# Half of a pair's VectorE background work put ahead of the pair's evacuation

## The chip, the cores and the metric

One core of one Trainium2 chip. The metric is the device time of the kernel in microseconds. A run of one core has no second die to compare with, so a run counts as fast when it is within 1.5% of the fastest of its kernel. Engines: PE is TensorE, DVE is VectorE, ACT is ScalarE, POOL is GpSimd, SP is SyncE.

## The reference

Input x is 2048 tokens of 576 features in bf16. It is normalised, and three things are added: x itself, a diagonal complex state-space layer (576 states, a scan over the 2048 tokens) and a gated unit with a hidden width of 4608.

```python
xn = _layernorm(x, axis=-1)
# _A_ref: Bu = xn @ B_bar^T (complex); h_t = Lam_bar * h_{t-1} + Bu_t; y = 2 Re(h C^T) + xn * Dskip
# _B_ref: (sigmoid(xn @ w_gate) * (xn @ w_up)) @ w_down
return x + _A_ref(xn, ...) + _B_ref(xn, ...)
```

## The kernel before

The tokens are four blocks of 512; two blocks make a half. For each half the hidden width is done in three slots of twelve 128-wide slices, so there are six stages. A stage first runs its **gate/up groups** (18 matmuls into one pair of PSUM banks, "pgu"; ACT makes a sigmoid and a copy, DVE multiplies them). Now and then a **state-input group** ("pbu") stands between them; ACT copies it into the SBUF tiles bure and buim. Then come the **down-projection pairs** ("pd"): two token tiles of 128 at a time, which DVE adds to an accumulator. In the third and sixth stage the pairs also carry the state terms and write the output.

All PSUM tiles rotate through four slots of two banks. Everything else that DVE has to do (tables, the scan, norms, residuals) is background work. It is a queue of items with estimated costs; at set points of the program `bg.step(us)` hands out credit, and as many items as the credit pays for are placed there in DVE's program.

```python
    def step(self, us):                      # class Background
        self.now += 1
        self.credit = min(self.credit + us, 5.0)
        while True:
            q = self.head()
            if q is None or q[0][0] > self.credit:
                return
            cost, fn, _ = q.popleft()
            self.credit -= cost
            fn()
# ... cut
psum = ctx.enter_context(tc.tile_pool(name="psum", bufs=PE_SLOTS, ...))    # PE_SLOTS = 4
# ... cut
        def evac(self):                      # class StateIn
            bre = ssmp.tile([P, TB], FP32, name="bure", tag="bure", bufs=2)
            bim = ssmp.tile([P, TB], FP32, name="buim", tag="buim", bufs=2)
            if self.pt < PT:
                nc.scalar.copy(bre[:], self.ps[:, 0, :])
                nc.scalar.copy(bim[:], self.ps[:, 1, :])
                bg.step(T_GROUP - 0.1)
# ... cut
    def ssm_w(nb, pt, part):                 # a background item; part 1 is the last reader of bre and bim
        bre, bim = bu[(nb, pt)]
        # ... cut
        a, b = (bre, bim) if part == 0 else (bim, bre)
        tq = bft("tq", 2)
        nc.vector.tensor_mul(w, t1, a[:])
        nc.vector.tensor_mul(tq[:], t2, b[:])
        # ... cut
# ... cut
    def d_pair(tts, terms, final, free=False):
        n = len(terms[0])                    # 12 terms; 21 in the stages with state terms
        pds = [ps_pair("pd") for _ in tts]
        # ... cut: the matmuls of the pair
        for tt, pd in zip(tts, pds):
            acc = accs[tt]
            if final:
                ob = lnp.tile([P, D], BF16, name="ob", bufs=2)
                nc.vector.tensor_add(halves(ob[:]), halves(acc[:]), pd[:, :, 0:DH])
                nc.sync.dma_start(o[tt * P:(tt + 1) * P, :], ob[:])
            else:
                nc.vector.tensor_add(halves(acc[:]), halves(acc[:]), pd[:, :, 0:DH])
        if free:
            acc_free[0] = tts[1] + 1
        for _ in tts:
            bg.step(n * T_DTERM - 0.76 - 0.2)
```

## Time and profile before

| | before |
|---|---|
| time, median of 3 runs | 507.96 us (507.86 to 508.02) |
| span of the profiled run | 505.8 us |
| PE busy | 499.5 us, 99% |
| DVE busy | 322.5 us, 64% |
| ACT busy | 204.5 us, 40% |
| PE's share of the chain that ended last | 98% |
| waits of PE that the trace names | 1.2 + 1.2 + 0.9 us |

How to read it: the chain is followed back from the last instruction, at each step to what released it. A kernel whose chain is 98% PE is as long as PE's work plus PE's gaps. Idle time on DVE counts only where PE or the end waits for it.

### The profile page before, as it was taken

The numbers are of one execution on the slowest core, as the hardware profiler recorded it, in microseconds if no ns is written. First come the engines' busy times: TensorE is split into PE (matmuls) and PEld (weight loads), VectorE is DVE, ScalarE is ACT, GpSimd is POOL, SyncE is SP. The second block draws the span as 40 slices with busy tenths as digits, with TensorE's granted clock in tenths as the row PEclk, the third lists the DMA queues.
The fourth block names the chain that finished last, engine by engine and source line by source line (L and its number), as shares of the span: only waits on it lengthen the run. The fifth ranks groups of instructions, "written<-read, shape, count | busy, mean of one in ns | idle before, by whom it ended". The sixth has DMA issues, their size and how long they took to land.

```text
span 505.8 us, 13370 instructions
## 1 busy us (share of the span) xinstructions
PE 499.5 (99%) x5892; PEld 311.6 (62%) x5892; DVE 322.5 (64%) x706; ACT 204.5 (40%) x368; POOL 90.8 (18%) x134
## 2 busy tenths in 40 slices
PE   8999999999999999999999999999999999999997
PEld 5544675444477444477764555985555985557995
DVE  6889679887868787847589767579675222221111
ACT  4955733556500756530025655005655005553000
POOL 7116320123200043110000331100431001300000
PEclk9999999999999999999999999999999999999999
DMA  8999694155220096232170661200643201600001
GB/s 212 208 162 247 134 192 100 27 139 141 49 49 27 2 189 155 61 88 73 48 143 1 165 141 49 49 16 10 162 103 88 50 25 30 184 1 1 26 25 49
DMA packets 40960, 45.77 MB, mean 90 GB/s; under 512 B 28614, under 2 KB 32326, under 8 KB 40902
## 3 DMA queue, kind: packets, MB, share of 16 engines
q0 software_dynamic: 10608, 34.22, 28.1%
q1 hardware_dynamic: 29862, 10.37, 11.0%
q8 instruction: 46, 0.75, 0.6%
q10 hardware_dynamic: 432, 0.33, 0.2%
q14 instruction: 12, 0.10, 0.1%
HBM read 34.36 MB, written 2.36 MB: 73 GB/s over the span
## 4 chain that ended last, share of the span: by engine, by line
PE 98%; DMA 1%; DVE 1%; ACT 0%; issue 0%; ACTq 0%
PE pgu L502 55%; PE pd L616 33%; PE pbu L531 7%; PE pd L576 1%; PE pd L584 1%; DMA xt<-in_A_x_dram 1%; PE ptr L780 0%; DVE bnst L230 0%; PE pgu L772 0%; ACT buim L538 0%; DVE xn L255 0%; DVE mv L231 0%; DVE ob L585 0%; PE ptr L196 0%; ACT bure L537 0%
## 5 line engine op out<-in xcount | busy, mean ns | idle before, releaser
L502 PE MATMUL pgu<-xT,wgu 64*128 64x512 bf16 (+1 forms) x2628 | 284.0, 373 | 1.2 <-ACT buim L538 1.2
L502 PEld LDWEIGHTS <-wgu 64*128 64x128 bf16 x2628 | 138.2, 94 | 141.5 <-issue 1.4
L616 PE MATMUL pd<-wd,hT 64*128 64x288 bf16 x2208 | 140.7, 283 | 0.0
L508 ACT ACTIVATE sT<-pgu 128x512 bf16<-128x512 f32 x144 | 86.5, 601 | 118.5 <-PE pgu L502 117.5
L616 PEld LDWEIGHTS <-hT 64*128 64x128 bf16 x2208 | 116.4, 94 | 20.0
L511 DVE TENSOR_TENSOR hT<-sT,uT 128x512 bf16<-128x512 bf16 x144 | 60.6, 422 | 84.3 <-ACT uT L509 84.2
L509 ACT CAST uT<-pgu 128x512 bf16<-128x512 f32 x144 | 84.2, 585 | 0.0
L154 POOL DMA_DIRECT2D wgu<-in_B_w_gate_dram x36 | 27.6, 766 | 228.4 <-PE pgu L502 216.6
L626 DVE TENSOR_TENSOR acc<-acc,pd 128x576 f32<-128x576 f32 x32 | 22.7, 750 | 35.9 <-PE pd L616 35.9
L160 POOL DMA_DIRECT2D wd<-in_B_w_down_dram x36 | 26.4, 735 | 104.5 <-PE pd L616 104.4
L537 ACT COPY bure<-pbu 128x512 f32<-128x512 f32 x16 | 9.4, 585 | 86.0 <-PE pbu L531 68.6
L623 DVE TENSOR_TENSOR ob<-acc,pd 128x576 bf16<-128x576 f32 x14 | 9.9, 751 | 41.8 <-PE pd L616 41.8
L531 PE MATMUL pbu<-xT,bt 64*128 64x512 bf16 x288 | 33.8, 376 | 0.0
L616 PEld LDWEIGHTS <-hst 64*128 64x128 bf16 x504 | 26.4, 94 | 4.5
L616 PE MATMUL pd<-ctre,hst 64*128 64x288 bf16 x224 | 28.8, 283 | 0.0
L616 PE MATMUL pd<-ctim,hst 64*128 64x288 bf16 x224 | 28.8, 283 | 0.0
L154 POOL DMA_DIRECT2D wgu<-in_B_w_up_dram x36 | 26.5, 737 | 1.8 <-DMA wgu<-in_B_w_up_dram 1.8
L445 DVE TENSOR_TENSOR_SCAN gre<-r,g0re,wrim 128x512 bf16<-128x512 f32 x20 | 25.6, 1279 | 0.1
L531 PEld LDWEIGHTS <-bt 64*128 64x128 bf16 x288 | 14.6, 94 | 15.9
L452 DVE TENSOR_TENSOR_SCAN gim<-r,g0im,wrim 128x512 bf16<-128x512 f32 x16 | 20.3, 1272 | 0.0
L230 DVE BATCH_NORM_STATS2 bnst<-xt 128x6 f32<-128x288 bf16 x32 | 12.5, 432 | 2.6 <-DMA xt<-in_A_x_dram 2.6
L432 DVE TENSOR_TENSOR tq<-T,buim 128x512 bf16<-128x512 bf16 x20 | 13.7, 685 | 0.0
(126 smaller groups left out, 292.9 us busy)
## 6 DMA issues: line engine op xcount, KB each, us to landing
wgu<-in_B_w_gate_dram POOLq DMA_DIRECT2D x36, 288.0 KB, 4.2
wgu<-in_B_w_up_dram POOLq DMA_DIRECT2D x36, 288.0 KB, 4.9
wd<-in_B_w_down_dram POOLq DMA_DIRECT2D x36, 288.0 KB, 4.9
out_dram<-ob SPq DMA_DIRECT2D x15, 144.0 KB, 1.9
xt<-in_A_x_dram SPq DMA_DIRECT2D x10, 144.0 KB, 3.4
xt<-in_A_x_dram POOLq DMA_DIRECT2D x4, 144.0 KB, 7.0
bt<-ctre POOLq DMA_DIRECT2D x2, 288.0 KB, 6.2
bt<-ctim POOLq DMA_DIRECT2D x2, 288.0 KB, 8.1
```

Source lines behind the costliest of these rows:

```text
L154: eng.dma_start(w[rows, :, :], src[:, fs].rearrange("(c p) f -> p c f", p=H))
L160: nc.gpsimd.dma_start(wd[:], B_w_down[f0:f0 + FP * P, :].rearrange("(n p) d -> p n d", p=P))
L432: nc.vector.tensor_mul(tq[:], t2, b[:])
L445: nc.vector.tensor_tensor_scan(gre[:], r_bc, w[:, 0, :], g0re[:, col], ALU.mult, ALU.add)
L452: nc.vector.tensor_tensor_scan(gim[:], r_bc, w[:, 1, :], g0im[:, col], ALU.mult, ALU.add)
L502: nc.tensor.matmul(self.ps[:, gi, cols], w[rows, c, fs], xT[self.nb][rows, c, cols], start=c == 0, stop=c == NH - 1)
L508: nc.scalar.activation(sT[:], self.ps[:, 0, :], ACT.Sigmoid)
L509: nc.scalar.copy(uT[:], self.ps[:, 1, :])
L511: nc.vector.tensor_mul(h[:], sT[:], uT[:])
L531: nc.tensor.matmul(out, w, xT[self.nb][rows, c, ts_], start=c == 0, stop=c == NH - 1)
L616: m = nc.tensor.matmul(pds[k][:, a, 0:DH], lhsT[rows, :], rhs[rows, a * DH:(a + 1) * DH], start=turn == 0 and i == 0, stop=turn == 1 and i ...
L626: nc.vector.tensor_add(halves(acc[:]), halves(acc[:]), pd[:, :, 0:DH])
```

## The change

The intent: in DVE's program the evacuation stands ahead of the background work, so in the kernel before DVE stands idle until the pair's matmuls are done and does its background work only afterwards. With one of the two steps ahead of the evacuation, that share fills the idle time.

```diff
+        bg.step(n * T_DTERM - 0.76 - 0.2)
         for tt, pd in zip(tts, pds):
             acc = accs[tt]
             if final:
@@
         if free:
             acc_free[0] = tts[1] + 1
-        for _ in tts:
-            bg.step(n * T_DTERM - 0.76 - 0.2)
+        bg.step(n * T_DTERM - 0.76 - 0.2)
```

## The prediction

> **What bounds the kernel now.** I read the engine totals first, then the chain of waits that ended last, then the waits of each engine, and last the timeline around the only gap that is left. The page of the kernel before:
>
> ```profile
> span 505.8 us, 13370 instructions
> PE 499.5 (99%) x5892; PEld 311.6 (62%) x5892; DVE 322.5 (64%) x706; ACT 204.5 (40%) x368; POOL 90.8 (18%) x134
> PEclk9999999999999999999999999999999999999999
> PE 98%; DMA 1%; DVE 1%; ACT 0%; issue 0%; ACTq 0%
> ```
>
> TensorE (PE) runs for 499.5 of 505.8 us at the full granted clock, and 98% of the chain is PE. VectorE (DVE) is busy 64% of the time and 1% of the chain. So the most that any reordering of VectorE work can win is PE's idle time, 505.8 - 499.5 = 6.3 us. The waits of PE say what it is made of:
>
> ```profile
> engine line waited for: us in total, times, longest us
> PE pgu L772 <- DVE warm L182: 1.2, 1, 1.2
> PE pgu L502 <- ACT buim L538: 1.2, 1, 1.2
> PE ptr L780 <- DVE rstd L238: 0.9, 1, 0.9
> ```
>
> Two of the three (1.2 and 0.9 us) lie in the first 7 us, before any pair. After PE's last matmul come about 3 us of last evacuation and store (505.8 - 502.9). That leaves one gap that background work can touch: 1.2 us, when a gate/up matmul of line 502 waited for ScalarE (ACT) to copy out "buim". 1.2 + 0.9 + 1.2 + 3.0 = 6.3, so nothing is left over.
>
> The waits of VectorE show why the change was thought of:
>
> ```profile
> DVE ob L623 <- PE pd L616: 41.8, 7, 8.9
> DVE acc L626 <- PE pd L616: 35.9, 14, 4.5
> ```
>
> VectorE sits idle 77.7 us at the evacuations of the down-projection pairs (lines 623 and 626), waiting for PE to finish the pair. But it is VectorE that waits; no row says that PE waits for these evacuations.
>
> Now the gap. The timeline of the three engines around it:
>
> ```profile
> 265.43 5.99 PE L502 MATMUL pgu<-xT,wgu 64*128 64x512 bf16 x54
> 272.58 3.63 PE L502 MATMUL pgu<-xT,wgu 64*128 64x512 bf16 x32 [1.15 <-ACT buim L538]
> ...
> 265.53 0.58 ACT L509 CAST uT<-pgu 128x512 bf16<-128x512 f32 x1
> 271.45 0.58 ACT L537 COPY bure<-pbu 128x512 f32<-128x512 f32 x1 [5.34 <-PE pgu L502]
> 271.93 0.59 ACT L538 COPY buim<-pbu 128x512 f32<-128x512 f32 x1
> ...
> 259.81 1.42 DVE L623 TENSOR_TENSOR ob<-acc,pd 128x576 bf16<-128x576 f32 x2 [1.04 <-PE pd L616]
> 261.15 0.45 DVE L270 TENSOR_TENSOR tmpxd<-xn,dskip_rows 128x576 bf16<-128x576 bf16 x1
> ...
> 265.80 0.42 DVE L476 TENSOR_TENSOR hst<-C,gre 128x512 bf16<-128x512 bf16 x1
> ...
> 268.06 0.68 DVE L431 TENSOR_TENSOR wrim<-T,bure 128x512 bf16<-128x512 bf16 x1
> ...
> 270.66 0.69 DVE L432 TENSOR_TENSOR tq<-T,bure 128x512 bf16<-128x512 bf16 x1
> ```
>
> ACT stood for 5.34 us before its copy into "bure". The trace names PE as the releaser, but the matmuls that fill this pbu had ended by 265.6 (265.43 is the start of the next group). There are two bure and two buim buffers; their last reader is the DVE multiply that starts at 270.66 and ends at 271.35, and ACT starts 0.10 us later. I therefore read it as a buffer wait on DVE. Behind it the four PSUM pair slots fill: one pbu uncopied and three gate/up groups, 265.6 to 271.44. The next group needs the pbu's slot, so PE stops at 271.44 until the second copy ends at 272.52. A late DVE costs PE 1.14 us here, once.
>
> [...] for a reordering only the gaps count, and the chain confirms that they are small. [...] of 23 pairs none makes PE wait. [...]
>
> **The change part by part.** A pair had: 2 evacuations, then two steps of background credit. Now it has: one step, 2 evacuations, one step. A step's credit is 12 x 0.245 - 0.96 = 1.98 us in ordinary stages and 21 x 0.245 - 0.96 = 4.185 us in the third stage's pairs, which carry the state terms too; unspent credit is kept up to 5.0. Nothing is removed and nothing added: the order listing has as many VectorE instructions as before, the same PE matmuls in the same order (only two wait lists differ), and ACT and GpSimd identical. What moves is one to three items from behind an evacuation to in front of it; SyncE issues a few loads and transposes earlier to match.
>
> Step one, the gap. In the third stage, pairs end at 228.9, 239.2, 249.5 and 259.8. The listing puts in front of the first evacuation one half-h (starts 230.28 to 231.41, so 1.13 us) and two w halves (1.66 and 1.67); in front of the second the two scans with their small followers (3.0) and four statistics tiles (3.8); in front of the third two residual-plus-norm tiles (1.93 each); in front of the fourth two more of those, two residual tiles (1.165 each) and one half-h. DVE walked through: free at 221.3, then 225.8, evacuation 228.94 to 230.3; 237.1, evacuation 239.23 to 240.6; 244.5, evacuation 249.5 to 250.9; 258.2, evacuation 259.81 to 261.15. All four stay on time. Behind the fourth, 2 x 1.165 + 1.13 = 3.46 us is now already done. The releasing multiply ends at 271.35 - 3.46 = 267.9 in place of 271.35, ACT's two copies end near 269.1 in place of 272.52, and PE wants that slot at 271.44. It is free 2.3 us early, so the whole gap goes: **minus 1.14 us**.
>
> ACT then has three groups to catch up: they cost about 0.96 us each in the trace when queued (272.41 to 273.36), so they end near 270.1, 271.0 and 272.4, ahead of PE's needs at 273.4, 275.3 and 277.3. No second gap follows.
>
> Step two, the other stages. In the first stage DVE is full: behind the first evacuation it does per-state work and a table half up to 67.7, and now the next table half (70.08 to 71.93, 1.85 us) as well, until 69.5. That pair ends at 68.74, so its evacuation is about 0.8 us late and ends near 70.9. The third pair's is about 0.5 late: 70.9 + 1.2 + 1.85 + 1.2 = 75.1 against 74.62. But a slot is used again one pair later, at 74.6 and 80.5. Both leave some 4 us: **0 us**. In the second stage the third evacuation is at most 0.2 late; in the fourth all are on time, DVE idling 0.98 to 3.16 us before each now. The fifth and sixth have no background work left, and the listing shows no move there: 0 us.
>
> Step three, the end and the start: unchanged, 0 us. Sum: 507.96 - 1.14 = 506.8 us.
>
> **The rivals.** (a) Late evacuations take the place of the wait: for it, DVE has 16.8 us of work in the 23.5 us first stage, and one late step there makes the next later; against it, the one-pair slack of 5.88 us is never more than a fifth used in my walk. If it happened in every pair of the first two stages I would see 1 to 3 us more, 509 to 511. (b) The gap stays because something else holds that group: it is the first to read the fourth block's transposed input, and its weight load waits for those transposes. Their median landing is 4.2 us and the last is issued at 258.8, so they should be there by about 263, and the change issues them earlier. If they were the true cause: 507.9. (c) The author's hope, that filling 77.7 us of VectorE idle shortens the kernel: against it, none of it is on the chain. It would need over 10 us of PE idle for 2%, and there are 6.3 in all.
>
> **Range and chances.** Runs of the kernel before lie within 0.16 us. Full removal gives 506.8, nothing removed 507.9, and a small gap elsewhere could give back a few tenths or bring 508.1. I take 506.8, range 506.4 to 508.0. Faster by 2% would need 497.8, below PE's busy time plus start and end; slower by 2% needs over 10 us of new stalls. 0.01 each.
>
> **What would show it.** PE's row "pgu <- buim 1.2" is gone, and PE's idle is near 5.1 us with busy still 499.5; ACT's 5.34 us wait shrinks to about 1.9 us (copy at 268.0 after 266.1). DVE's busy stays at 322.5 while its idle before evacuations falls, most at the first pair of the third stage (7.65 to about 3.2). In the first stage the second and third evacuations start some 0.8 and 0.5 us after their pair. I am wrong if PE shows a wait at a pd or pgu group for an evacuation, if that gap stays with a transpose named, or if the span moves by more than 2 us.

The costs of the walk are those that the traces show (the evacuation 749 ns, the multiplies that read bure and buim 685 ns), and the sum stands as forecast, 507.96 - 1.14 = 506.8 us.

## The result, and the profile after

The changed kernel took 506.38 us (median of 6 runs, 505.89 to 506.77), the kernel before 507.87 us (6 runs, 507.38 to 508.02). The ratio is 0.9971, with a 95% interval of 0.9959 to 0.9984. Ratios here are the mean time of one kernel's fast runs over that of the other's fast runs of the same rounds, so not quite the ratio of the medians. The forecast was 506.8 us with a range of 506.4 to 508.0; 506.38 lies just under it. The gain of about 1.4 us is larger than the 1.14 forecast.

The page of the changed kernel, the totals and the chain by engine:

```profile
span 504.9 us, 13370 instructions
PE 500.5 (99%) x5892; PEld 290.6 (58%) x5892; DVE 323.3 (64%) x706; ACT 204.7 (41%) x368; POOL 91.0 (18%) x134
PE 99%; DVE 0%; ACT 0%; issue 0%
```

Its waits, of PE first, then of DVE at the evacuations (now lines 624 and 627); the columns are total us, times, longest us:

```profile
PE pgu L772 <- DVE warm L182: 1.3, 1, 1.3
...
DVE ob L624 <- PE pd L616: 38.3, 7, 8.9
DVE acc L627 <- PE pd L616: 30.2, 12, 4.5
```

The row in which a gate/up group waited for the copy into buim is gone, and PE has no wait left but one at the start. DVE's idle time at the evacuations fell by 9.2 us (77.7 to 68.5), while the kernel gained less than a sixth of that. The timeline of the changed kernel where the gap had been (start, length, engine, line, operation, and in brackets the idle time before it with its releaser):

```profile
265.80 10.52 PE L502 MATMUL pgu<-xT,wgu 64*128 64x512 bf16 x96
...
268.36 0.59 ACT L537 COPY bure<-pbu 128x512 f32<-128x512 f32 x1 [1.89 <-DVE tq L432]
268.84 0.59 ACT L538 COPY buim<-pbu 128x512 f32<-128x512 f32 x1
...
260.18 1.42 DVE L624 TENSOR_TENSOR ob<-acc,pd 128x576 bf16<-128x576 f32 x2 [1.54 <-PE pd L616]
...
267.57 0.69 DVE L432 TENSOR_TENSOR tq<-T,bure 128x512 bf16<-128x512 bf16 x1
```

PE runs through in one block. The fourth evacuation is on time. The multiply that frees bure ends at 268.26, which is 8.1 us after the start of that evacuation; before, it was 11.5 us (259.81 to 271.35). The trace now names DVE as what ACT waited for, as the prediction had read it.

Where the difference arises is best seen in the chain in order of time (start, length, what). Before:

```profile
265.60 5.85 PE pgu L502 x54
...
271.93 0.60 ACT buim L538
...
272.58 7.95 PE pgu L502 x72
```

After:

```profile
265.96 13.60 PE pgu L502 x126
```

The seven groups from 265.60 ended at 280.53 before, 14.93 us in all; after, they take 13.60. **That is 1.33 us, not 1.14.** Everything else is equal to a hundredth, as one more reading shows. I call *main part* the time from the first long block of gate/up matmuls (450 in a row) to the last evacuation of the chain (line 585):

| profiled run | block starts | last evacuation | main part |
|---|---|---|---|
| before | 11.15 | 502.92 | 491.77 |
| changed | 11.52 | 501.96 | 490.44 |

The difference is 1.33 us again. The start differs by 0.37 us between these two runs, to the disadvantage of the changed kernel. The runs below show that it does so from run to run whatever the kernel.

### The profile page after: what moved, and what is told of

Same layout as the page of the kernel before. It is cut to its first block, busy times and chain, and to the rows that moved or that the text cites. A ratio compares the mean times of both kernels' runs of the same rounds, so it can differ in the third digit from the quotient of the medians.

```text
span 504.9 us, 13370 instructions
## 1 busy us (share of the span) xinstructions
PE 500.5 (99%) x5892; PEld 290.6 (58%) x5892; DVE 323.3 (64%) x706; ACT 204.7 (41%) x368; POOL 91.0 (18%) x134
## 4 chain that ended last, share of the span: by engine, by line
PE 99%; DVE 0%; ACT 0%; issue 0%
PE pgu L502 55%; PE pd L616 33%; PE pbu L531 7%; PE pd L576 1%; PE pd L584 1%; PE pgu L772 1%; PE ptr L780 0%; ACT xT L783 0%; DVE xn L255 0%; DVE xT L783 0%; DVE ob L585 0%; DVE warm L182 0%; DVE rstd L238 0%; DVE eps_t L178 0%; DVE zero_t L180 0%
## 5 line engine op out<-in xcount | busy, mean ns | idle before, releaser
L502 PEld LDWEIGHTS <-wgu 64*128 64x128 bf16 x2628 | 128.1, 94 | 150.4
L616 PEld LDWEIGHTS <-hT 64*128 64x128 bf16 x2208 | 107.6, 94 | 28.7
L616 PEld LDWEIGHTS <-hst 64*128 64x128 bf16 x504 | 24.5, 94 | 6.3
```

The lines of the kernel that those rows point to most:

```text
L502: nc.tensor.matmul(self.ps[:, gi, cols], w[rows, c, fs], xT[self.nb][rows, c, cols], start=c == 0, stop=c == NH - 1)
L616: m = nc.tensor.matmul(pds[k][:, a, 0:DH], lhsT[rows, :], rhs[rows, a * DH:(a + 1) * DH], start=turn == 0 and i == 0, stop=turn == 1 and i ...
```

## The experiments

The theory: the change wins only in the third stage, by letting DVE free bure and buim earlier there. ACT then copies the pbu in time, and PE does not run out of PSUM slots. Rivals: (a) the gain is spread over the stages; (b) the group waited for its transposed input, which the change also loads earlier; (c) late evacuations cost something, so that the change gains and loses at once; (d) the start or something else of the build differs. A last question was size: why 1.33 and not 1.14. Twelve runs were made, all with correct results. The diffs are against the changed kernel unless said otherwise.

### The third stage alone, and all but the third

```diff
-        bg.step(n * T_DTERM - 0.76 - 0.2)
+        ahead = n > FC            # others_only: n == FC
+        if ahead:
+            bg.step(n * T_DTERM - 0.76 - 0.2)
@@
-        bg.step(n * T_DTERM - 0.76 - 0.2)
+        for _ in range(1 if ahead else 2):
+            bg.step(n * T_DTERM - 0.76 - 0.2)
```

> The step ahead of the evacuation is kept only in the four pairs of the third stage; elsewhere both steps stay behind. Theory (the late release of the bure/buim buffers after the third stage is the only thing that the change removes): the whole gain, about 1.4 us, TensorE's 1.2 us wait for the copy into buim gone. Rival (the gain is spread over all stages, or comes from the start): well under 1 us here.

> The complement: the step ahead in all stages but the third. Theory: no gain, 507.9 us, the wait for the copy into buim still there at 1.2 us. Rival (spread over all stages, or a start that the new build makes shorter): a good part of 1.4 us.

The two kernels split the change cleanly: DVE's program in third_only differs from the kernel before only in the third stage, and in others_only only in the other stages (the sixth has no background work left). Measured: third_only 506.63 us against 507.69, ratio 0.9976 (0.9964 to 0.9989), main part 490.44. others_only 507.77 us, ratio 1.0002 (0.9989 to 1.0016), main part 491.77. PE's waits in others_only:

```profile
PE pgu L775 <- DVE warm L182: 1.3, 1, 1.3
PE pgu L502 <- ACT buim L538: 1.1, 1, 1.1
```

So the whole gain sits in four of the 23 pairs, and rival (a) falls. In the other 19 the change wins nothing: the twelve of the first, second and fourth stage move work into time that nobody waits for, and the seven of the fifth and sixth stage have no background work to move.

### The same release without touching the pairs

Against the kernel before; the diff is:

```diff
                 queue_ln(3, 0)
                 queue_ln(2, 2)
-                queue_ln(3, 2)
@@
+            if slot == 3:
+                run_groups([GateUp(slot, f, nb) for (f, nb) in order[:12]])
+                order = order[12:]
+                queue_ln(3, 2)
             run_groups([GateUp(slot, f, nb) for (f, nb) in order])
```

> The kernel before, pairs untouched; only the four residual tiles of the last block (4.65 us of VectorE work in front of the releasing multiply) are queued twelve groups later. Theory (VectorE's lateness in freeing bure and buim holds ScalarE, and ScalarE holds TensorE): the gap goes, gain about 1.3 us as with the change. Rival (the group waits for its transposed input, or it is the order of evacuation and background work itself that counts): no gain.

Measured: 506.79 us against 507.69, ratio 0.9979 (0.9967 to 0.9992), main part 490.52, PE's gap gone. ACT's wait at this place in the trace:

```profile
ACT bure L537 <- DVE tq L432: 0.4, 1, 0.4
```

The pairs stand as before, the transposes of the fourth block are issued as before, and still the gap goes once four residual tiles no longer stand ahead of the releasing multiply. Rival (b) falls. The trace of the kernel before says so too: the last of these transposes is issued at 258.8 and the slowest of the four lands 4.4 us after its issue, long before the matmul that waited until 272.58. This kernel also moves two state-input groups among the gate/up groups, one of them to the very place of the gap. The main part is 0.08 us longer than with the change, and that is a small gap of the same kind: one pair of matmuls starts at 278.49, 0.07 us later than it was due, just after the last copy into buim has ended at 278.44.

### Both steps ahead

```diff
-        bg.step(n * T_DTERM - 0.76 - 0.2)
+        for _ in tts:
+            bg.step(n * T_DTERM - 0.76 - 0.2)
         for tt, pd in zip(tts, pds):
@@
-        bg.step(n * T_DTERM - 0.76 - 0.2)
```

> Both steps of every pair ahead of the evacuation. Theory: evacuations of the first stages start up to 2 us late, but a pair's slots are needed one pair (5.88 us) later, so no TensorE wait; the gap stays gone: like the change, 506.4 us, within 0.3. Rival (late evacuations become the new wait): TensorE waits at pd groups, 0.5 to 3 us slower than the change.

Measured: 506.08 us against 507.69, ratio 0.9969 (0.9956 to 0.9981), main part 490.44. The first evacuation of the first stage in the timeline:

```profile
64.77 1.42 DVE L628 TENSOR_TENSOR acc<-acc,pd 128x576 f32<-128x576 f32 x2
```

Its pair ended at 62.72 (stage start 56.84 plus a quarter of 23.52), so it is 2.05 us late, and PE does not wait. The median is the lowest of all runs, but the main part is that of the change to the hundredth. Its block starts at 11.05 against 11.52 in the profiled run of the change. So I do not call it faster.

### How late may DVE be: idle work behind the fourth evacuation

The changed kernel with k multiplies that nobody reads, placed behind the evacuation of the third stage's fourth pair:

```diff
+    def spin(k):
+        for _ in range(k):
+            junk = ssmp.tile([P, D], BF16, name="junk", tag="tq", bufs=2)
+            nc.vector.tensor_mul(junk[:], dskip_rows[:], dskip_rows[:])
@@
+        pairs_seen[0] += 1
@@
+        if pairs_seen[0] == 12:
+            spin(k)
         if free:
```

> The changed kernel with 5 idle VectorE multiplies (about 1.85 us) put behind the fourth evacuation of the third stage. The profile of the change leaves 2.37 us between ScalarE's last copy (269.43) and TensorE's need (271.80). Theory: no wait, time as the change (main part 490.44 us). Rival (no slack: each microsecond of VectorE lateness costs TensorE): 1.8 us slower.

> The same with 10 multiplies (about 3.7 us). Theory: the lateness beyond 2.37 us comes back as a gap of about 1.3 us at the same matmul, released by the copy into buim, and the main part grows by 0.2 us more than the gap that the trace shows (1.5 us), as it shrank by 1.33 for a shown gap of 1.14. Rival (lost time equals shown gap): 1.3.

> The same with 17 multiplies (about 6.3 us). Theory: shown gap about 3.9 us, main part longer by about 4.1: a fixed 0.2 on top of the shown gap. Rival (the excess is a share of the gap, 17%): 4.6.

| k | time, median | of before, same rounds | gap shown | main part | over 490.44 |
|---|---|---|---|---|---|
| 5 | 506.37 | 507.43 | none | 490.44 | 0 |
| 10 | 507.82 | 507.43 | 1.38 | 491.99 | 1.55 |
| 17 | 512.15 | 507.43 | 3.96 | 496.26 | 5.82 |

A lateness of about 1.85 us (five multiplies at the 0.37 us of behind_10, an estimate), within the slack of 2.37, is free. At k = 10 and 17 the same gap comes back at the same matmul, with the same releaser, and about as long as the multiplies exceed the slack (3.68 - 2.37 = 1.31 us and 6.26 - 2.37 = 3.89). This is a dial on the cause: the gap opens and closes with DVE's lateness alone. The excess of the loss over the shown gap is 0.17 us at k = 10 (1.55 - 1.38) and 0.18 in the kernel before (1.33 - 1.15). At k = 17 it is 1.86, which neither reading expected. The windows of behind_17 say why (window, its length, then busy us of PE, PEld, DVE, ACT and POOL with instructions, granted clock of PE, DMA share, GB/s):

```profile
275.00:276.00 1.00, 0.58 (x6) 0.33 (x7) 0.84 (x1) 1.00 (x3) 0.00 (x0) 0.98 0.00 0
276.00:277.00 1.00, 1.00 (x8) 0.38 (x4) 0.61 (x2) 1.00 (x3) 0.00 (x0) 0.50 0.00 0
277.00:278.00 1.00, 1.00 (x8) 0.50 (x6) 1.00 (x1) 1.00 (x3) 0.00 (x0) 0.50 0.00 0
278.00:279.00 1.00, 1.00 (x8) 0.44 (x6) 0.96 (x7) 0.31 (x1) 0.00 (x0) 0.50 0.00 0
279.00:280.00 1.00, 1.00 (x10) 0.50 (x8) 0.97 (x4) 0.99 (x2) 0.00 (x0) 0.82 0.00 0
```

After a gap of 3.96 us the clock is halved (0.50) for about 3.4 us (the shortfalls of the column: 0.02 + 3 x 0.50 + 0.18 = 1.70 us of full clock). So 3.96 + 0.17 + 1.70 = 5.83, against 5.82 measured. In behind_10 the clock stays at 1.00 after its 1.38 us (windows from 272.5 to 280).

### How late may an evacuation be

The changed kernel with k idle multiplies ahead of the second evacuation of the fifth stage, which has no background work (`if pairs_seen[0] == 18: spin(k)` ahead of the loop over the evacuations).

> The changed kernel with 33 idle VectorE multiplies (about 12.2 us) ahead of the second pair's evacuation in the fifth stage, where there is no background work. VectorE can start them after the first evacuation (about 397.3), so the second ends near 410.9; its slots are wanted by the fourth pair at 408.2. Theory (one pair of slack): TensorE waits about 2.8 us there, released by the evacuation, about 3 us slower. Rival (slots wanted only later, or sooner): no wait, or 5.9 us more.

> As the run with 33, but 22 multiplies (about 8.1 us): the second evacuation of the fifth stage starts some 3.5 us after its pair has ended and ends near 406.8, before the fourth pair wants the slots at 408.2. Theory (a late evacuation within one pair is free): main part as the change, 490.44 us. Rival (late evacuations cost): 1 to 3.5 us slower.

With 33: 511.27 us against 507.43, main part 495.47. PE's wait:

```profile
PE pd L624 <- DVE acc L637: 3.0, 2, 2.6
```

The two parts are 2.58 us before the first matmul of the fourth pair and 0.39 after it; the second tile's evacuation frees its slot later. After that the clock was at 0.50 again for some 3.4 us (0.78, 0.50, 0.50 and 0.51 in the four microseconds from 410, a shortfall of 1.71 us of full clock). So an idle time of 2.58 us, one matmul and 0.39 us more was enough for it here. With 1.7 us for the clock, the rest of the loss is 5.03 - 1.7 = 3.3 us, the 3.0 shown plus 0.3; two restarts at the 0.17 us of behind_10 would be 0.34, an estimate.

With 22, three runs took 506.15 to 506.61 us, but the fourth, the profiled one, took 1371.72 us. Its trace shows matmuls almost three times as far apart from beginning to end (5.32 us a group in place of 1.94), so it says nothing of the wait. ACT and DVE kept their usual durations (597 ns a sigmoid and 425 ns a multiply of the gate/up groups, against 601 and 422 in the kernel before), and its page has no line for the granted clock. It came once, and its cause is open.

> The run with 22 multiplies once more, since its profiled execution was one of 1371 us and says nothing of the wait. Theory: no wait of TensorE at a down-projection group, main part 490.44 us, time as the change; the second evacuation starts some 3 us after its pair. Rival: TensorE waits, 1 to 3.5 us slower.

Measured: 506.25 us against 507.43, ratio 0.9973, main part 490.44, and no wait of PE at a pair. DVE's timeline:

```profile
397.23 8.20 DVE L604 TENSOR_TENSOR junk<-dskip_rows 128x576 bf16<-128x576 bf16 x22
405.33 1.43 DVE L637 TENSOR_TENSOR acc<-acc,pd 128x576 f32<-128x576 f32 x2
407.65 1.42 DVE L637 TENSOR_TENSOR acc<-acc,pd 128x576 f32<-128x576 f32 x2 [0.90 <-PE pd L624]
```

The third evacuation, on time, starts at 407.65, so the second pair had ended at about 401.77 (407.65 - 5.88), and its evacuation was 3.6 us late for nothing. Rival (c) falls: an evacuation 3.6 us late, within one pair's time of 5.88 us, was free; the one of late_33, 7.7 us late (409.24 against 395.64 + 5.88 = 401.52), cost PE 3.0 us of waits.

### Both kernels once more

> The changed kernel once more, for the size. Theory: main part 490.44 us again, against 491.77 of before, so a true gain of 1.33 us, with start and end varying by half a microsecond from run to run. Rival (the change wins 1.5 us or more by something beside the gap): main part shorter than 490.44.

> The kernel before against itself, to see what the start and the end do without any change: ratio 1.000, single runs between 507.2 and 508.2, main part 491.77 us, and a first full matmul block that starts anywhere between 11.0 and 11.5 us.

Measured: the changed kernel 506.37 us (506.17 to 506.76) against 507.6, ratio 0.9976 (0.9963 to 0.999). The kernel before against itself: 507.54 (507.43 to 508.12), ratio 1.0001, main part 491.77. The block of the first started at 10.91, of the second at 10.92. The main part of after_again was 490.73, not 490.44. It is longer rather than shorter, so it gives the rival (d) nothing. Set beside the first profile of the change, matmul by matmul, 0.08 of the 0.29 arise at 17.97 us, where one pair of matmuls starts 0.28 us after the one before (0.22 elsewhere) with no wait named, and the other 0.21 at the start and the end of the sixth stage's pairs. Why that run lost this I cannot say.

All runs of the kernel before, 43 with the first three, lie between 507.19 and 508.16 with a mean of 507.63; the 11 of the changed kernel between 505.89 and 506.77 with a mean of 506.37. The difference is 1.26 us, in keeping with the 1.33 of the traces. Part of the spread may go with the clock at the start: in the first profile of the change, whose block starts at 11.52, the packed trace records the full clock from 6.8 us on, in that of the kernel before (11.15) from 4.4 us on. No run tests this.

## Why the prediction was right or wrong

- **What bounds the kernel, and that DVE's idle time is not on the chain: right.** 68.5 us of it remain, and PE waits for none of it.
- **The cause of the gap (buffer wait of ACT on DVE, against the releaser that the trace named): right,** shown by the dial of behind_5, behind_10 and behind_17 and by resid_later.
- **The walk through the third stage: right.** ACT's wait was forecast at about 1.9 us and is 1.89. The idle time before the stage's first evacuation was forecast at about 3.2 and is 3.19. The slack was forecast at 2.3 and is 2.37 (269.43 to 271.80).
- **The other stages, 0 us: right** (others_only). Of the late evacuations of the first stage, the second is 0.8 us late as forecast. The third is at 75.73 where its pair ended at 74.95 (57.31 + 17.64), so 0.8 late where 0.5 was forecast.
- **"minus 1.14 us": the mechanism right, the size wrong.** This is the term that failed: it took the gap as it is drawn, from 271.44 to 272.58, for the time lost. The loss was 1.33 us. The matmuls run in pairs, one of gate and one of up; the trace starts a pair every 216 ns (1.943 us / 9), but draws each matmul 376 ns long. Here are the last pair before the gap and the first behind it:

```profile
271.04 0.38 PE L502 MATMUL pgu<-xT,wgu 64*128 64x512 bf16 x2
272.58 0.39 PE L502 MATMUL pgu<-xT,wgu 64*128 64x512 bf16 x2 [1.15 <-ACT buim L538]
```

After 271.044 (the start of the upper line to the nanosecond) the next pair was due at 271.260 and came at 272.578, so 1.32 us late. In behind_10 the same count gives 271.271 and 272.810, so 1.54 us late of 1.55 lost. The drawn gap misses the 160 ns (376 - 216) by which the last matmul's drawn end lies beyond the start that was due. So the excess is accounted for to 0.01 us in both traces.

- **The base and the range: the base too high, the range too narrow.** The prediction took 507.96 from three runs that lay within 0.16 us, and gave its low end 0.4 us. The 43 runs have a mean of 507.63 and spread over 1.0 us, with first blocks starting between 10.7 and 11.5 us in the profiled runs of all these kernels. So the base was 0.33 us too high, more than the 0.19 by which the gap was mis-sized, and both lie on the same side. With 507.63 and 1.33 the sum would have been 506.30; the 11 runs of the changed kernel have a mean of 506.37.
- **"PE's idle is near 5.1 us with busy still 499.5": wrong as a sign.** PE's busy time read 500.5, since the 16 idle warm-up matmuls at the start took 5.09 us in that run and 4.19 in the run of before; its idle time read 4.4. Busy time of PE is no steady ruler to a microsecond here; the main part is.
- **PE's weight loads (PEld), 62% on the page before: a wrong reading, on which no term rests.** The prediction took the 62% to say that the matmul work could be packed better. The share counts overlapping loads once; summed, the loads take 556.7 us before and 557.6 after, 110% of the span, so the 62% says nothing of room left. The share is not steady either: 62% before and 58% after, for 5892 loads each. From 423 to 460 us, all gate/up work at 1.94 us a group, loads are busy for 19.58 of 37 us before and 16.70 after. In these traces the share is higher behind the gap: in the kernel before it is 2.53 of 5.80 us just ahead of it (265.60 to 271.40) and 12.71 of 24 us behind it (285 to 309), where the changed kernel, without the gap, has 10.83.
- **The prediction's three rivals:** late evacuations and the transposes were given little weight, and both fell. Filling idle time of DVE for its own sake won nothing, as said.

## What to carry to other kernels

On a kernel whose chain is one engine, list that engine's few gaps and ask of each which chain of buffers leads to it; moving work on another engine helps only where it shortens that chain, here four pairs of 23. In these traces a gap in a stream of overlapping matmuls cost more than its drawn length (0.17 us more at 1.38 us, 0.18 at 1.15), so count it from start to start; behind a long one (3.96 us) the clock was halved as well, at 0.50 for about 3.4 us. So a slack that holds the gap at zero is worth more than it looks. Before giving a range of a few tenths of a microsecond, take the spread from more than three runs.
